# Polysketch attention and a rational feed-forward layer on one core: other product counts per unit, bfloat16 ones, and a new order from step 178 on

## The chip, the cores and the metric

The kernel runs on one core of one Trainium2 chip. A core has a matrix engine (TensorE; PE in the profile, with PEld for its weight loads), a vector engine (VectorE, DVE), a scalar engine (ScalarE, ACT), GpSimd (POOL) and SyncE (SP), and 16 DMA engines. The engines run side by side, each takes its own instructions strictly in order, and they wait for each other through semaphores. The metric is the device time of one execution, in microseconds (us); lower is better. Before the change it is 257.98 us, the median of 3 runs (257.85 to 258.45).

## The reference

Two layers. The first is linear attention with product features, for 4 batches, 4 heads, 1088 positions and head size 32:

```python
def phi(x):
    a = einsum('rd,bhsd->bhsr', S1, x)      # r = 8
    b = einsum('rd,bhsd->bhsr', S2, x)
    return einsum('bhsi,bhsj->bhsij', a, b).reshape(*x.shape[:-1], 64)
q_p, k_p = phi(q), phi(k)
kv, z = einsum('bhsf,bhsd->bhfd', k_p, v), sum(k_p, axis=2)
x = einsum('bhsf,bhfd->bhsd', q_p, kv) / (einsum('bhsf,bhf->bhs', q_p, z)[..., None] + 1e-06)
```

Its result is laid out as 4352 tokens of 128 numbers and goes through a feed-forward layer with 2048 hidden numbers per token and a rational activation:

```python
h = x @ w_in
P = a[0] + a[1] * h + a[2] * h**2 + a[3] * h**3
Q = 1.0 + abs(b[0]) * abs(h) + abs(b[1]) * h**2
out = (P / (Q + 1e-06)) @ w_out
```

## The kernel before

**Units.** The feed-forward layer is cut into 21 units (`UNITS`): a stretch of 256 or 512 tokens and some of the 16 blocks of 128 hidden numbers. Units 3 to 17 have 4096 numbers on each of 128 partitions, the others 1024 or 2048. The steps of unit i are named in a long string, `ORDER`, as a letter, the unit's number and a part:

- H: TensorE computes a 1024-wide part of h in PSUM, in fp32 (`hidden`, L511; a wide unit has four parts; the buffer `h_ps` exists twice). E copies it to SBUF as bfloat16 `hh` (`evac`, L517, on ScalarE).
- U, W, Y: u = |h| by masking the sign bit (L524), w = ab1·u + ab0 (L538), w = w·u (L553), on VectorE; then L and X on ScalarE give r = exp(-ln(w + 1 + 1e-6)), which is 1/Q (L575, L579).
- P, V, S, G on VectorE: g = a3·h + a2 (L558; on ScalarE at L561 where the step ends in `.a`), g = g·h (L571), s = h·r (L583), g = g·s (L587).
- Or, Os, Og: TensorE multiplies r, s and g with `w_out` scaled by a0, by a1 and unscaled, and adds all of it up in one PSUM tile for the token stretch (`gather`, L616). Each is one "product term", 32 matmuls of 128x128 in a wide unit.

**Three variants.** In a unit of the list `TWO` the step A adds a1 to g, so that the term with s falls away and two terms are left. The addition is a DMA that accumulates: GpSimd issues two transfers that add `ones`, a DRAM tile filled with a1, to g (`plus`, L567). In a unit of the list `FOUR` there is no P, V or G; B and C compute h²·r and h³·r (L592, L599), and four terms are summed with `w_out` scaled by a0 to a3 (w6 and w7 make two of those tables). In a unit of `SQ` (and `ABS`, the same units) ScalarE computes w = ab1·h² (D, `square`, L543, two halves) and u = ab0·|h| (L530), and the step M adds u to w by two accumulating DMAs (`join`, L549); W on VectorE and Y are absent, and so is U.

**Attention.** Steps K (keys of a batch) and Q (a stretch of queries) build the features and the result. On TensorE their steps s, sk and p write only 64 of the 128 output partitions with each matmul; they are called half-width here, and all other steps of TensorE full-width. The steps c, k, pl, kk are small copies from PSUM that run on ScalarE (`.a`) or VectorE (`.d`), f, r and x run on VectorE, b is a transpose on TensorE; dw and dr send sketches through DRAM on SP's queue.

**Order.** `ORDER` is written out by hand or by a program ahead of time and is issued step by step, under manual scheduling; so the order of the instructions on each engine, and that of SP's and GpSimd's DMAs, is the order of this string. ST copies a finished PSUM tile to SBUF (`turn_out`), OUT stores it from SP's queue (L653; the last one L645). AB prepares |b| and its root, AW writes `ones`, w0 to w5 scale and cast `w_out` in halves, Z are idle matmuls.

Of the kernel before, what the change touches and what calls it, by code (L numbers as in the profile page):

```python
# [22 lines left out]
TWO = (6, 7, 8, 10, 12, 14, 15)  # L23
SQ = (5, 9, 13)
ABS = (5, 9, 13)
FOUR = (11, 13, 16, 17)
# [3 lines left out]
WIDE = {'U': 4096, 'W': 4096, 'Y': 4096, 'V': 4096, 'S': 4096, 'G': 4096, 'L': 4096}  # L30
# [38 lines left out]
C13.0 U15.0 P15.1.d W15.0 V15.0 Y15.0 H16.0 Or13.0 H16.1 E16.0 A14.0 E16.1 X14.0 Q3.2.b H16.2 H16.3 Os13.0
Q3.2.kk.d E16.2 E16.3 L15.0 OUT10 A15.0 S14.0 U16.0.d W16.0.d G14.0 Y16.0 Or14.0 H17.0 H17.1 E17.0 E17.1 X15.0  # L70
On13.0 H17.2 H17.3 Om13.0 Og14.0 S15.0 E17.2 E17.3 U17.0.d G15.0 W17.0.d Y17.0 L16.0 H18.0 ST14.a H18.1 Or15.0
X16.0 E18.0 E18.1 L17.0 OUT14 OUT12 S16.0 X17.0 U18.0.d B16.0 W18.0.d C16.0 Y18.0 Og15.0 H19.0 Or16.0 Os16.0
Om16.0 On16.0 E19.0 L18.0 ST16.a U19.0.a X18.0 W19.0.a S17.0 B17.0 P18.0.d H20.0 C17.0 Y19.0 P19.0.a E20.0 L19.0
Or17.0 Om17.0 Os17.0 On17.0 OUT16 X19.0 ST17.a V18.0 P20.0.a U20.0.d V19.0 W20.0.d S18.0 Y20.0 S19.0 G18.0 V20.0
L20.0 Z4 Or18.0 OUT17 X20.0 Or19.0 Os18.0 Os19.0 Og18.0 Or20.0 S20.0 Os20.0 G19.0 Og19.0 G20.0 Og20.0 ST20 OUT20
# [4 lines left out]
def kernel(  # L80
# [164 lines left out]
    root1 = consts.tile([128, 1], FP, name="root1")  # L245
# [3 lines left out]
    a1, a2, a3 = a_sb[:, 1:2], a_sb[:, 2:3], a_sb[:, 3:4]  # L249
# [240 lines left out]
    def span(i, stage, k):  # L490
        w = END if i == NU - 1 and stage in "LXSG" else WIDE.get(stage, 2048)
        return k * w, min((k + 1) * w, width(i))
# [22 lines left out]
    def evac(i, part):  # L515
        c, ce = part * HW, min((part + 1) * HW, width(i))
        nc.scalar.copy(out=at(i, "hh", c, ce), in_=live[i]["h", part][:, :ce - c])  # L517
# [9 lines left out]
    def d_w(i, k, eng="d"):  # L527
        c = span(i, "W", k)
        if i in ABS:
            nc.scalar.activation(out=at(i, "u", *c), in_=at(i, "hh", *c), func=ACT.Abs, scale=ab0)  # L530
# [7 lines left out]
        nc.vector.tensor_scalar(out=at(i, "w", *c), in0=at(i, "u", *c), scalar1=ab1, scalar2=ab0,  # L538
                                op0=AX.mult, op1=AX.add)

    def square(i, k):
        c = span(i, "D", k)
        nc.scalar.activation(out=at(i, "w", *c), in_=at(i, "hh", *c), func=ACT.Square, scale=root1)  # L543
# [127 lines left out]
    def w_part(x, eng):  # L671
        if x >= 6:
            t = feature_tile(x - 6)[:, 0:4].rearrange("p t h i j -> p (t h i j)").bitcast(BF)
            t = w_sb[x - 3] = t.rearrange("p (f d) -> p f d", f=nf)
            if eng == "d":
                nc.vector.tensor_scalar(out=t, in0=w_sb[2], scalar1=a_sb[:, x - 4:x - 3], scalar2=None, op0=AX.mult)
            else:
                nc.scalar.activation(out=t, in_=w_sb[2], func=ACT.Copy, scale=a_sb[:, x - 4:x - 3])
# [7 lines left out]
        if y == 2:  # L686
            copy(eng, o, t)
        elif eng == "d":
            nc.vector.tensor_scalar(out=o, in0=t, scalar1=a_sb[:, y:y + 1], scalar2=None, op0=AX.mult)
        else:  # L690
            nc.scalar.activation(out=o, in_=t, func=ACT.Copy, scale=a_sb[:, y:y + 1])

    def written(_):
        nc.sync.dma_start(out=ones.rearrange("p (a c) -> p a c", c=128),
                          in_=a1_sb[:, None, :].broadcast_to([128, 16, 128]))

    def absolute(_):
        if TWO:
            nc.gpsimd.tensor_copy(out=a1_sb, in_=a1.broadcast_to([128, 128]))
        nc.scalar.activation(out=b_abs, in_=b_sb, func=ACT.Abs)  # L700
        if SQ:
            nc.scalar.activation(out=root1, in_=ab1, func=ACT.Ln, bias=tiny)
            nc.scalar.activation(out=root1, in_=root1, func=ACT.Exp, scale=0.5)
# [6 lines left out]
              "On": lambda i, k: gather(i, 4, k), "B": d_h2, "C": d_h3, "ST": turn_out, "OUT": store, "F": fetch, "I": early, "w": w_part, "Z": turn, "AB": absolute, "AW": written, "SS": sketch_weights}  # L710
# [44 lines left out]
```

## Time and profile before

| what | value |
|---|---|
| time, median of 3 runs | 257.98 us |
| span of the profiled execution, first to last instruction | 255.8 us |
| the profiled execution's own time | not on the page; the runs' median lies 2.2 us above the span |
| busy PE / DVE / ACT / POOL | 249.8 / 243.3 / 232.2 / 22.5 us |
| granted TensorE clock | 1.000 |
| product terms on PE (L616), share of the chain | 33.8% |
| hidden parts on PE (L511), share of the chain | 47.3% |
| accumulating transfers: `ones` into g | 14 of 512 KB, median 9.7 us from issue to landing |
| accumulating transfers: u into w | 6 of 512 KB, median 6.9 us |

The chain is the sequence of work that ended last, followed back from the last instruction; its share by line says how much of the span each line holds. Busy times of different engines overlap. A group's mean duration is the time from an instruction's start to its end; the next one on the same engine can start a little before that end. Half of PE's first 15 us are idle matmuls and short attention steps, and the last 4 us are the output's copy and store.

### The profile page before, as it was taken

How to read it: one execution, taken by the hardware profiler on the slowest of the kernel's cores; microseconds unless marked ns; L12 is line 12 of the kernel's file. 1: busy time of each engine (PE TensorE's matmuls, PEld its weight loads, DVE VectorE, ACT ScalarE, POOL GpSimd, SP SyncE). 2: the span in 40 equal slices, each digit the busy share in tenths (PEclk: the TensorE clock that was granted, in tenths of full speed). 3: DMA queues.
4: the chain of work that ended last, by engine and by line, in shares of the span. 5: the costliest groups of instructions: out<-in, count | busy, mean ns of one | idle time of the engine just before them, and what ended most of it. 6: DMA issues, size and time to landing. Idle time of an engine off the chain costs nothing.

```text
span 255.8 us, 6273 instructions
## 1 busy us (share of the span) xinstructions
PE 249.8 (98%) x2699; PEld 178.0 (70%) x2702; DVE 243.3 (95%) x242; ACT 232.2 (91%) x176; POOL 22.5 (9%) x46
## 2 busy tenths in 40 slices
PE   8999999999999999999999999999999999999993
PEld 3677746646866575666756656689566599999982
DVE  3699999999999999999999999999999999999992
ACT  2179989999999999999999999999899899999980
POOL 4000000000300040202200100220002020000000
PEclk9999999999999999999999999999999999999999
DMA  6999375649884669395995695399008575120100
GB/s 189 278 324 259 108 219 158 149 86 292 192 193 133 196 135 124 74 112 85 152 140 146 140 117 97 35 143 190 6 0 93 75 86 81 31 54 3 44 23 21
DMA packets 22618, 31.85 MB, mean 125 GB/s; under 512 B 2880, under 2 KB 15808, under 8 KB 22592
## 3 DMA queue, kind: packets, MB, share of 16 engines
q0 software_dynamic: 2880, 10.49, 30.1%
q1 hardware_dynamic: 19424, 20.90, 29.5%
q8 instruction: 21, 0.34, 0.5%
q10 hardware_dynamic: 288, 0.08, 0.1%
q14 instruction: 5, 0.04, 0.0%
HBM read 31.39 MB, written 4.26 MB: 139 GB/s over the span
## 4 chain that ended last, share of the span: by engine, by line
PE 96%; ACT 1%; DVE 0%; issue 0%; DVEq 0%
PE h_ps L511 47%; PE out_ps L616 34%; PE att_ps L426 3%; PE out_ps L197 3%; PE att_ps L330 2%; PE att_ps L454 2%; PE att_ps L299 1%; PE att_ps L366 1%; PE h_ps L376 1%; PE h_ps L299 1%; ACT hh L517 0%; ACT ln L575 0%; ACT w_out L265 0%; PE att_ps L197 0%; PE att_ps L322 0%
## 5 line engine op out<-in xcount | busy, mean ns | idle before, releaser
L511 PE MATMUL h_ps<-xT,w_in_sb 128*128 128x512 f32 (+1 forms) x320 | 126.2, 537 | 0.0
L511 PEld LDWEIGHTS h_ps<-xT,w_in_sb 128*128 128x128 f32 x320 | 57.5, 190 | 41.7 <-issue 36.6
L517 ACT CAST hh<-h_ps 128x1024 bf16<-128x1024 f32 x68 | 69.3, 1045 | 3.7 <-PE h_ps L511 2.2
L575 ACT ACTIVATE ln<-w 128x4096 f32<-128x4096 bf16 (+2 forms) x21 | 63.1, 3006 | 0.2 <-DVE w L553 0.2
L579 ACT ACTIVATE r<-ln 128x4096 bf16<-128x4096 f32 (+2 forms) x21 | 63.0, 2999 | 0.1
L583 DVE TENSOR_TENSOR s<-hh,r 128x4096 bf16<-128x4096 bf16 (+2 forms) x21 | 39.5, 1883 | 0.3 <-ACT r L579 0.2
L616 PEld LDWEIGHTS <-r 128*128 128x128 bf16 x544 | 31.7, 98 | 6.0 <-issue 5.1
L616 PEld LDWEIGHTS <-g 128*128 128x128 bf16 x544 | 31.4, 98 | 5.8 <-issue 5.1
L616 PE MATMUL out_ps<-w_out,r 128*128 128x128 bf16 x544 | 33.7, 219 | 0.0
L553 DVE TENSOR_TENSOR w<-w,u 128x4096 bf16<-128x4096 bf16 (+2 forms) x18 | 32.5, 1806 | 0.1
L571 DVE TENSOR_TENSOR g<-g,hh 128x4096 bf16<-128x4096 bf16 (+2 forms) x17 | 30.3, 1783 | 0.0
L587 DVE TENSOR_TENSOR g<-g,s 128x4096 bf16<-128x4096 bf16 (+2 forms) x17 | 30.2, 1781 | 0.0
L616 PEld LDWEIGHTS <-s 128*128 128x128 bf16 x448 | 25.9, 98 | 3.6 <-issue 3.4
L616 PE MATMUL out_ps<-w_out,g 128*128 128x128 bf16 x416 | 26.0, 219 | 0.0
L567 POOL DMA_DIRECT2D g<-ones x14 | 13.8, 1157 | 103.7 <-PE out_ps L616 39.1
L616 PE MATMUL out_ps<-w_out,s 128*128 128x128 bf16 x320 | 19.8, 219 | 0.0
L538 DVE TENSOR_SCALAR w<-u,b_abs 128x4096 bf16<-128x4096 bf16 (+2 forms) x17 | 19.3, 1136 | 0.0
L558 DVE TENSOR_SCALAR g<-hh,a_sb 128x2048 bf16<-128x2048 bf16 (+1 forms) x24 | 19.0, 793 | 0.0
L524 DVE TENSOR_SCALAR u<-hh 128x4096 uint16<-128x4096 uint16 (+2 forms) x17 | 17.3, 1015 | 0.1
L543 ACT ACTIVATE w<-hh,root 128x2048 bf16<-128x2048 bf16 x6 | 12.2, 2031 | 0.0
L549 POOL DMA_DIRECT2D w<-u x6 | 5.4, 1058 | 74.4 <-ACT u L530 74.4
L530 ACT ACTIVATE u<-hh,b_abs 128x4096 bf16<-128x4096 bf16 x3 | 11.1, 3713 | 0.0
(81 smaller groups left out, 207.1 us busy)
## 6 DMA issues: line engine op xcount, KB each, us to landing
g<-ones POOLq DMA_DIRECT2D x14, 512.0 KB, 9.7
w<-u POOLq DMA_DIRECT2D x6, 512.0 KB, 6.9
a_all<-sk_d SPq DMA_DIRECT2D x6, 352.0 KB
b_all<-sk_d SPq DMA_DIRECT2D x12, 176.0 KB
v_sb<-in_v_dram SPq DMA_DIRECT2D x12, 144.0 KB
k_sb<-in_k_dram SPq DMA_DIRECT2D x3, 544.0 KB
q_sb<-in_q_dram SPq DMA_DIRECT2D x3, 544.0 KB
out_dram<-out_sb SPq DMA_DIRECT2D x19, 64.0 KB
```

The lines of the kernel that those rows point to most:

```text
L511: nc.tensor.matmul(t[:, (x - part * m) * tl:(x - part * m + 1) * tl], lhsT=w_in_sb[:, (f0 + x) * 128:(f0 + x + 1) * 128], rhs=xT[:, p:p + ...
L517: nc.scalar.copy(out=at(i, "hh", c, ce), in_=live[i]["h", part][:, :ce - c])
L524: nc.vector.tensor_scalar(out=at(i, "u", *c).bitcast(U16), in0=at(i, "hh", *c).bitcast(U16), scalar1=0x7FFF, scalar2=None, op0=AX.bitwise_and)
L538: nc.vector.tensor_scalar(out=at(i, "w", *c), in0=at(i, "u", *c), scalar1=ab1, scalar2=ab0, op0=AX.mult, op1=AX.add)
L553: nc.vector.tensor_mul(out=at(i, "w", *c), in0=at(i, "w", *c), in1=at(i, "u", *c))
L558: nc.vector.tensor_scalar(out=at(i, "g", *c), in0=at(i, "hh", *c), scalar1=a3, scalar2=a2, op0=AX.mult, op1=AX.add)
L571: nc.vector.tensor_mul(out=at(i, "g", *c), in0=at(i, "g", *c), in1=at(i, "hh", *c))
L575: nc.scalar.activation(out=ln_sb[:, :ce - c], in_=at(i, "w", c, ce), func=ACT.Ln, bias=1.0 + 1e-6)
L579: nc.scalar.activation(out=at(i, "r", c, ce), in_=ln_sb[:, :ce - c], func=ACT.Exp, scale=-1.0)
L583: nc.vector.tensor_mul(out=at(i, "s", *c), in0=at(i, "hh", *c), in1=at(i, "r", *c))
L587: nc.vector.tensor_mul(out=at(i, "g", *c), in0=at(i, "g", *c), in1=at(i, "s", *c))
L616: nc.tensor.matmul(outs[t0][:, m * 128:(m + 1) * 128], lhsT=z[:, m * 128:(m + 1) * 128], rhs=w, start=first and j == 0 and m == 0, stop=le ...
```

## The change

- **Lists.** `TWO` goes from units 6, 7, 8, 10, 12, 14, 15 to 7 and 9 to 15; `SQ` from 5, 9, 13 to 6, 8, 10, 12, 14; `FOUR` from 11, 13, 16, 17 to 16, 17. `ABS` goes. So there are 8 x 2 + 5 x 2 = 26 accumulating transfers instead of 7 x 2 + 3 x 2 = 20.
- **Squared units.** u is now |h| from VectorE's U, unscaled, ScalarE computes only the square (one 4096-wide instruction, scaled so that w is ab1/ab0·h²), M adds them, and the factor ab0 moves into the scale operand of Ln. `RT` computes the new root, with a guard for ab0 near zero (`scale0`, on GpSimd).
- **`ones` in bfloat16.** It holds a1 rounded to bfloat16. So that the sum is still right, a2 and a3 are multiplied by rounded a1 over a1, and the unscaled table of `w_out` by the inverse (`KA0` to `KA2`: small operations on GpSimd, with one reciprocal on VectorE between them). w4 and w5 become scaled casts.
- **P** is one 4096-wide instruction instead of two halves (but for unit 3).
- **Moves.** E14.1 and E14.2 run on VectorE; some output copies, w7 and small copies change between VectorE and ScalarE.
- **Order.** The first 178 steps are the old ones with RT and KA put in behind AB; everything behind them is in another order, with parts of H in other sequences within a unit (for example H5.3, H5.2, H5.0, H5.1).

The core of the diff:

```diff
-TWO = (6, 7, 8, 10, 12, 14, 15)
-SQ = (5, 9, 13)
-ABS = (5, 9, 13)
-FOUR = (11, 13, 16, 17)
+TWO = (7, 9, 10, 11, 12, 13, 14, 15)
+SQ = (6, 8, 10, 12, 14)
+FOUR = (16, 17)
+HALF = (3,)
...
-WIDE = {'U': 4096, 'W': 4096, 'Y': 4096, 'V': 4096, 'S': 4096, 'G': 4096, 'L': 4096}
+WIDE = {'U': 4096, 'W': 4096, 'Y': 4096, 'V': 4096, 'S': 4096, 'G': 4096, 'L': 4096, 'P': 4096, 'D': 4096}
...
-K1.f0 AB0 w0.a w4.a K1.c1.d F1.q K1.f1 E0.0 U0.0 H1.0 Q0.3.sk E1.0 F1.v Q0.2.dr Q0.1.p H2.0 P0.0.d Q0.3.c.d W0.0
+Q0.0.r Q0.0.x K1.T2 Q0.2.c.a Z2 Q0.0.b K1.s1 I6 I10 Q0.2.dw Q0.1.f K1.c0.a Q0.3.T Q0.0.kk.a H0.0 w2.d K1.f0 AB0 RT0
+w0.a KA0 KA1 KA2 w4.a K1.c1.d F1.q K1.f1 E0.0.a U0.0.d H1.0 Q0.3.sk E1.0.a F1.v Q0.2.dr Q0.1.p H2.0 P0.0.d Q0.3.c.d
...
-L20.0 Z4 Or18.0 OUT17 X20.0 Or19.0 Os18.0 Os19.0 Og18.0 Or20.0 S20.0 Os20.0 G19.0 Og19.0 G20.0 Og20.0 ST20 OUT20
+V18.0 Or17.0 ST17.a U20.0.d V19.0 W20.0.d Y20.0 S18.0 Or18.0 X19.0 Or19.0 S19.0 G19.0 G18.0 OUT17 Os18.0 Og19.0
+P20.0.a V20.0 Os19.0 Og18.0 L20.0 X20.0 Or20.0 S20.0 G20.0 OUT14 Os20.0 Og20.0 ST20 OUT20
...
-        a1_sb = consts.tile([128, 128], FP, name="a1_sb")
-        ones = dram.tile([128, 2048], FP, name="ones", bufs=1)
+        a1_sb = consts.tile([128, 256], BF, name="a1_sb")
+        ones = dram.tile([128, 2048], BF, name="ones", bufs=1)
...
-        if i in ABS:
-            nc.scalar.activation(out=at(i, "u", *c), in_=at(i, "hh", *c), func=ACT.Abs, scale=ab0)
-            return
...
-        nc.scalar.activation(out=at(i, "w", *c), in_=at(i, "hh", *c), func=ACT.Square, scale=root1)
+        nc.scalar.activation(out=at(i, "w", *c), in_=at(i, "hh", *c), func=ACT.Square, scale=root)
...
-        nc.scalar.activation(out=ln_sb[:, :ce - c], in_=at(i, "w", c, ce), func=ACT.Ln, bias=1.0 + 1e-6)
+        nc.scalar.activation(out=ln_sb[:, :ce - c], in_=at(i, "w", c, ce), func=ACT.Ln, bias=1.0 + 1e-6,
+                             scale=scale0 if i in SQ else 1.0)
...
+        by = k_inv if y == 2 else a_sb[:, y:y + 1]
...
     def absolute(_):
-        if TWO:
-            nc.gpsimd.tensor_copy(out=a1_sb, in_=a1.broadcast_to([128, 128]))
         nc.scalar.activation(out=b_abs, in_=b_sb, func=ACT.Abs)
-        if SQ:
-            nc.scalar.activation(out=root1, in_=ab1, func=ACT.Ln, bias=tiny)
-            nc.scalar.activation(out=root1, in_=root1, func=ACT.Exp, scale=0.5)
+        nc.gpsimd.tensor_scalar(out=scale0, in0=ab0, scalar1=1e-12, scalar2=None, op0=AX.max)
+
+    def nearest(n):
+        if n == 0:
+            nc.gpsimd.tensor_copy(out=a1_sb, in_=a1.broadcast_to([128, 256]))
+            nc.gpsimd.tensor_scalar(out=zero, in0=a1_sb[:, 0:1], scalar1=0.0, scalar2=None, op0=AX.is_equal)
+            nc.gpsimd.tensor_add(out=near[:, 0:1], in0=a1, in1=zero)
+            nc.gpsimd.tensor_add(out=near[:, 1:2], in0=a1_sb[:, 0:1], in1=zero)
+        elif n == 1:
+            nc.vector.reciprocal(out=near_inv, in_=near)
+        else:
+            nc.gpsimd.tensor_mul(out=a_k[:, 0:1], in0=near[:, 1:2], in1=near_inv[:, 0:1])
+            nc.gpsimd.tensor_mul(out=a_k[:, 1:2], in0=near[:, 0:1], in1=near_inv[:, 1:2])
+            nc.gpsimd.tensor_mul(out=a_k[:, 2:4], in0=a_sb[:, 2:4], in1=a_k[:, 0:1].broadcast_to([128, 2]))
+
+    def square_root(_):
+        nc.scalar.activation(out=ln_b[:, 0:1], in_=scale0, func=ACT.Ln)
+        nc.scalar.activation(out=ln_b[:, 1:2], in_=ab1, func=ACT.Ln, bias=tiny)
+        nc.scalar.mul(ln_b[:, 0:1], ln_b[:, 0:1], -0.5)
+        nc.scalar.activation(out=root, in_=ln_b[:, 1:2], func=ACT.Exp, scale=0.5, bias=ln_b[:, 0:1])
```

More of the change, by code (lines that the diff above doesn't have):

```diff
@@ L69 @@
[L69 to L73, printed above, removed]
@@ L490, in span @@
     def span(i, stage, k):
[L491 removed]
+        w = END if i == NU - 1 and stage in "LXSG" else 2048 if stage == "P" and i in HALF else WIDE[stage]
         return k * w, min((k + 1) * w, width(i))
@@ L675, in w_part @@
             if eng == "d":
-                nc.vector.tensor_scalar(out=t, in0=w_sb[2], scalar1=a_sb[:, x - 4:x - 3], scalar2=None, op0=AX.mult)
+                nc.vector.tensor_scalar(out=t, in0=w_sb[2], scalar1=a_k[:, x - 4:x - 3], scalar2=None, op0=AX.mult)
             else:
-                nc.scalar.activation(out=t, in_=w_sb[2], func=ACT.Copy, scale=a_sb[:, x - 4:x - 3])
+                nc.scalar.activation(out=t, in_=w_sb[2], func=ACT.Copy, scale=a_k[:, x - 4:x - 3])
             return
@@ L685, in w_part @@
             return
[L686 to L689, printed above, removed]
+        by = k_inv if y == 2 else a_sb[:, y:y + 1]
+        if eng == "d":
+            nc.vector.tensor_scalar(out=o, in0=t, scalar1=by, scalar2=None, op0=AX.mult)
         else:
-            nc.scalar.activation(out=o, in_=t, func=ACT.Copy, scale=a_sb[:, y:y + 1])
+            nc.scalar.activation(out=o, in_=t, func=ACT.Copy, scale=by)
```

85 lines of the change are left out of this document (46 added, 39 removed).

## The prediction

> **What bounds the kernel now.** I read the page's totals first, then the table of busy time per stretch, then the chain that ended last, then single instructions around the two places that the change touches outside the main run (its head and its tail).
>
> ```profile
> span 255.8 us, 6273 instructions
> ...
> PE 249.8 (98%) x2699; PEld 178.0 (70%) x2702; DVE 243.3 (95%) x242; ACT 232.2 (91%) x176; POOL 22.5 (9%) x46
> ```
>
> Three engines are over 90% busy, so the totals do not say which one sets the end. The stretches do (window: length, then PE, PEld, DVE, ACT, POOL busy):
>
> ```profile
> 12.79:25.60 12.81, 12.65 (x127) 9.85 (x128) 12.48 (x27) 10.50 (x17) 0.00 (x0) 1.00 0.96 291
> ...
> 115.11:127.90 12.79, 12.79 (x178) 9.00 (x177) 12.79 (x12) 12.79 (x8) 3.50 (x4) 1.00 0.76 119
> ...
> 179.06:191.80 12.74, 12.74 (x99) 7.77 (x98) 12.47 (x11) 11.68 (x8) 0.07 (x1) 1.00 0.02 3
> 191.85:204.60 12.75, 12.75 (x88) 7.48 (x86) 12.72 (x9) 11.52 (x8) 1.64 (x2) 1.00 0.68 84
> ...
> 243.01:255.80 12.79, 8.50 (x135) 7.55 (x133) 8.20 (x13) 5.93 (x8) 0.00 (x0) 1.00 0.08 22
> ```
>
> From 38 to 243 us PE has no hole, DVE is idle for about 1.1 us in all, ACT for about 3.1 us, most of it in the two stretches at 179 to 205. So PE sets the end, DVE is right behind it and ACT a little further: whatever is taken from one engine is worth only what the other two can follow. The chain agrees; it is PE work laid end to end:
>
> ```profile
> 99.84 1.79 PE out_ps L616 x32
> ...
> 103.28 3.63 PE h_ps L511 x8
> 106.92 1.79 PE out_ps L616 x32
> 108.70 3.49 PE h_ps L511 x8
> ```
>
> One product term of a 4096-wide unit (32 matmuls at L616) is 1.79 us. Two hidden-layer parts (8 instructions) take 3.49 us behind a full-width step and 3.63 us behind a half-width one.
>
> The head, where the change adds instructions, and two DVE rows for the spacing:
>
> ```profile
> 16.87 1.13 ACT L691 ACTIVATE w_out<-ln,a_sb 128x1024 bf16<-128x1024 f32 x1
> 17.91 1.03 ACT L265 CAST w_out<-ln 128x1024 bf16<-128x1024 f32 x1
> 18.85 1.00 ACT L517 CAST hh<-h_ps 128x1024 bf16<-128x1024 f32 x1
> ...
> 19.99 0.42 DVE L524 TENSOR_SCALAR u<-hh 128x1024 uint16<-128x1024 uint16 x1
> ```
>
> ACT runs w0, w4 and E0.0 in a row, and DVE's U0.0 starts 0.14 us after E0.0 has ended: it waits for it. Costs of the operations (mean ns last before the idle column):
>
> ```profile
> L558 DVE TENSOR_SCALAR g<-hh,a_sb 128x2048 bf16<-128x2048 bf16 x23 | 18.5, 804 | 0.0
> L538 DVE TENSOR_SCALAR w<-u,b_abs 128x4096 bf16<-128x4096 bf16 x12 | 16.1, 1341 | 0.0
> L524 DVE TENSOR_SCALAR u<-hh 128x4096 uint16<-128x4096 uint16 x12 | 14.7, 1221 | 0.1
> L543 ACT ACTIVATE w<-hh,root 128x2048 bf16<-128x2048 bf16 x6 | 12.2, 2031 | 0.0
> L530 ACT ACTIVATE u<-hh,b_abs 128x4096 bf16<-128x4096 bf16 x3 | 11.1, 3713 | 0.0
> L592 DVE TENSOR_TENSOR g<-s,hh 128x4096 bf16<-128x4096 bf16 x4 | 9.2, 2289 | 0.0
> ```
>
> Neighbours overlap by 0.09 us on DVE (a product that starts at 204.18 is followed at 206.38, 2.20 us later, though it lasts 2.29) and by 0.10 on ACT, so I count a product as 2.20, U as 1.14, W as 1.25, half a P as 0.72, an evacuation as 0.95, Abs as 3.6, half a square as 1.93.
>
> **The change, engine by engine.** PE: units with two products go from seven to eight (7, 9 to 15), with four from four to two (16, 17). Among the 15 wide units that was 7x2 + 4x4 + 4x3 = 42 terms and becomes 8x2 + 2x4 + 5x3 = 39: three terms fewer, 3 x 1.79 = -5.4 us. Grouping: I counted the unbroken runs of half-width steps in both orders: 19 before, 18 after. A run costs about 0.15 us on the way in (Q.p for three tiles 0.85 us instead of 0.70 in the chain) and 0.14 on the way out, so -0.3 us. Hidden parts, attention steps and idle matmuls (Z) are the same in number.
>
> DVE, in us: U in three more units (the squared units now take it) +3.4; W in two fewer -2.5; Y in two fewer -4.4; V and G in two more (units 11, 13) +8.8; B and C in two fewer -8.8; P from 10 units at 2 x 0.72 to 12 at one 4096-wide instruction, priced as W's 1.25 (same operation and shape), +0.6; two evacuations of unit 14 moved here +2.4 (by the PSUM copies, 0.385 us for 256 and 0.690 for 512, some 1.2 for 1024); the smaller moves (three output copies, w7 and P18 to ACT, three key copies, P19 and Q3.0.kk back, three xT copies away, den steps, one reciprocal) -2.7. Sum -3.2.
>
> ACT: three Abs away -10.8; squares from 6 x 1.93 to five 4096-wide at 3.64 (the 4096-wide Abs) +6.6; two evacuations away -1.9; output copies +1.3; w7 +1.85 (as a 2048-wide row); P18 and P19 +0.9; xT copies +0.75; small copies -0.4; a per-partition scale on five Ln and on w4, w5 +0.6 (the scaled w0 took 1.13 us where plain w4 took 1.03); two more root steps +0.4. Sum -0.7. ACT is hardly relieved.
>
> POOL and the queues: 26 accumulating transfers instead of 20, each two issues of about 1 us on an engine that is 9% busy; the extra 6 cost POOL time that nobody waits for. `ones` becomes bfloat16, so an A transfer reads half as much and should land like an M (median 6.9 us, not 9.7). SP: OUT14, with 6 stores, is now behind OUT17. Stores issue 0.43 us apart, OUT17's began at 245.5, so 10 of them end near 249.8 before any shift, ahead of the last store's 251.95: no cost; without that 2 us of cover it would delay the end by up to 2.6.
>
> **The head.** RT0 puts two more tiny ACT steps and a POOL round trip (scale0) ahead of w0.a; dependent tiny ACT steps are 0.32 us apart (16.44, 16.76), so w0 starts near 17.4 instead of 16.87. w4.a now waits for KA2: POOL's chain of small operations (0.1 to 0.3 us each by its rows), then a reciprocal on DVE that queues behind K1.f0 until 18.3, then three POOL multiplies, so about 18.95 instead of 17.91. Queued behind w4 are E0.0 (end 20.95 instead of 19.85) and E1.0, which today waits 0.40 us for PE and swallows that much. ACT, packed from 21 us on, runs +0.65; U0.0 waits, DVE +0.9; PE takes the +0.65 over near 28 us, where it already waits for ACT's kvz copy. Bounds: 0 (added steps give nothing back) and +1.1, with every POOL step at the 0.29 of its 128-wide copy. I take 0.65, since the short rows are the nearer ones.
>
> **The tail.** After the last X, DVE still has two G; now S20 and one G, -0.6 us for DVE and ACT's end. PE needs no credit.
>
> **Sum.** PE -5.4 - 0.3 + 0.65 = -5.0. DVE -3.2 + 0.9 - 0.6 = -2.9, or -4.0 if its 1.1 us of idle closes. ACT -0.7 + 0.65 - 0.6 = -0.65, or -3.75 if all 3.1 us of its idle closes. So ACT decides. Its idle at 179 to 205 (1.06 + 1.23 us) lay where PE worked off the four-product units 11 and 13 and kept it waiting for h_ps. Those are gone: for a pair of units 10 to 15 (one squared, one not) PE now needs 2 x (6.97 + 3.58) = 21.1 us and ACT 25.4, so ACT is not starved there; I close these 2.3 us and leave the other 0.8. Then -0.65 - 2.3 = -2.95 on the span of 255.8, that is 252.85. The page gives no time for the profiled execution but its span; the median of 257.98 lies 2.2 us above it, which the change doesn't touch: 257.98 - 2.95 = 255.0 us. Bounds of the sum: with the head at 0 and all ACT idle closed -4.4, with the head at 1.1 and none closed -0.2.
>
> **A rule against it.** POOL's issue rows while DVE was full:
>
> ```profile
> L549 POOL DMA_DIRECT2D w<-u x6: 857/1100/1220, 66.8 to 171.2; - x6
> ...
> DMA to landing us min/median/max: 4.6/6.9/9.1
> ```
>
> The two issues of one A ran from 145.85 to 147.61 across a DVE product that began at 146.51 and lasted 2.29, and neither was late. The Trainium skill (SBUF — State Buffer, "Who interferes with whom") states that a DVE operation in a two-port mode and a GpSimd operation lock each other out for a whole instruction, descriptor writing included. By that rule the held POOL of rival 3 would be the normal case, and the time 262.2 instead of 255.0; the trace does not agree in this place, and the landings above were taken beside a full DVE, so the sum goes by the rows.
>
> **Rivals.** (1) PE alone decides: ACT finds work all the time, the head hides. -3.75 to -5.0, so 254.2 to 253.0. For it: in the new order PE's work summed up to each step (rows times counts) stays ahead of DVE's by 2 to 8 us and of ACT's by 2 to 12. Against it: ACT would have to run without a hole from 21 us to the end. (2) ACT's holes only move (fewer hidden parts ready, a wait for DVE's Y instead): -0.65 to 0, so 257.3 to 258. Against: 25.4 against 21.1. (3) Slower: the joins land late. Five Ln now wait for an M on the fullest engine. Between the end of D and its Ln the order has 11.5 (unit 6), 11.4, 11.4, 10.1 (unit 12) and 11.4 us of ACT work. M needs one issue plus a landing: 1.1 + 6.9 at the median, 10.2 at the slowest M, but 13.5 at the slowest A row (12.4). At that row units 12 and one other stall 3.4 + 2.1 = 5.5 us, so 255.0 + 5.5 = 260.5; it decides from some 3 us of such stalls on. Against: 6.9 leaves 2 us spare. The same would come about if POOL were held for a whole product at each issue: 1.1 + 6.9 + 2 x 2.29 = 12.6 us, 7.2 us of stalls over the five, 262.2; the issues from 145.85 speak against it, and it has 0.02 of this rival's chance. (4) The grouping does nothing: 0.3 us, inside all the others.
>
> **How the numbers follow.** Forecast 0.50, with its own range 254.2 to 256.4; rival 1 0.20; rival 2 (up to 258.3) 0.16; rival 3 0.14. A measurement here tells about 0.2%, 0.5 us, from no change. Faster by more (under 257.5): 0.50 + 0.20 + 0.07 of rival 2 = 0.77; the same 0.09; slower 0.14. Range: 253.0, rival 1's end, to 258.2, rival 2's.
>
> **What would show it.** PE's L616 rows 96 matmuls fewer and PE's holes some 2 us in all after 38; ACT's busy time about 231.5 and no hole over 0.5 us between 150 and 215; P at 4096 in one row near 1.34; the Ln of units 6, 8, 10, 12, 14 with no DMA ahead of it; E0.0 starting near 20.0. Wrong if a wait for w (a join) or for g (ones) shows ahead of Ln or G, if ACT waits for h_ps as long as before, or if the head costs over 1.1.

## The result and the profile after

| | changed kernel | the same again | kernel before beside them |
|---|---|---|---|
| median time | 255.99 us (5 runs, 255.07 to 256.81) | 255.30 us (6 runs, 254.87 to 255.59) | 258.02 and 257.67 us |
| ratio to before, 95% interval | 0.9918 [0.9890, 0.9946] | 0.9898 [0.9876, 0.9920] | 1 |
| span of the profiled execution | 253.3 us (its time 255.07) | 253.1 us (its time 254.87) | 255.8 us |

The change makes the kernel faster by 0.8 to 1.0%, that is by 2.0 to 2.4 us on the medians. The forecast was 255.0 us with an own range of 254.2 to 256.4: both medians lie in it, 0.3 and 1.0 us above the forecast.

The changed kernel's page, its span, its busy time per engine and its chain by engine:

```profile
span 253.3 us, 6086 instructions
...
PE 244.4 (96%) x2603; PEld 172.1 (68%) x2606; DVE 240.1 (95%) x229; ACT 231.9 (92%) x179; POOL 32.9 (13%) x59
...
PE 38%; ACT 21%; DVE 19%; issue 13%; DMA 6%; SPq 1%; ACTq 0%; DVEq 0%
```

PE has lost 5.4 us of work, DVE 3.2, ACT 0.3, and the span only 2.5. The chain was PE to 96% before. Now it is PE from some 30 to 113 us (ahead of that it runs over loads and attention steps) and then changes hands, as its pieces in order of time (start, length, what) show:

```profile
109.42 1.79 PE out_ps L618 x32
111.21 1.79 PE h_ps L518 x4
113.05 0.59 DVE s L585
...
118.87 2.10 DVE g L572
120.97 2.30 DVE w L554
...
130.77 3.52 ACT ln L576
...
135.07 3.63 ACT r L581
```

The table by stretch for the changed kernel (window: length, then PE, PEld, DVE, ACT, POOL busy). The first two rows cut the main run in two, the others are the places where ACT was starved before and where it is now:

```profile
38.40:115.00 76.60, 76.60 (x767) 49.66 (x766) 76.02 (x71) 74.61 (x58) 6.33 (x6) 1.00 0.59 148
115.00:205.00 90.00, 88.98 (x866) 58.92 (x866) 89.06 (x67) 89.76 (x56) 21.57 (x20) 1.00 0.71 138
...
179.06:191.80 12.74, 12.69 (x115) 8.44 (x115) 12.74 (x9) 12.74 (x7) 4.51 (x4) 1.00 0.45 86
191.85:204.60 12.75, 12.54 (x116) 8.37 (x114) 12.56 (x8) 12.75 (x10) 3.59 (x5) 1.00 1.04 197
51.16:63.90 12.74, 12.74 (x98) 7.14 (x96) 12.74 (x14) 11.59 (x11) 0.00 (x0) 1.00 0.42 130
63.95:76.70 12.75, 12.75 (x161) 8.43 (x159) 12.75 (x12) 12.09 (x11) 0.00 (x0) 1.00 0.52 130
```

At 179 to 205 ACT now runs without a hole, where it was idle for 2.3 us before. But at 51 to 77 it is idle for 1.15 + 0.66 = 1.8 us, where before it was idle for 0.03. PE is still full there, and ACT waits for its hidden parts; ACT's instructions in that place (start, length, what, idle time before):

```profile
52.10 3.62 ACT L581 ACTIVATE r<-ln 128x4096 bf16<-128x4096 f32 x1 [0.26 <-PE out_ps L618]
...
58.90 1.01 ACT L272 CAST hh<-h_ps 128x1024 bf16<-128x1024 f32 x1 [0.69 <-PE h_ps L518]
...
66.45 1.01 ACT L272 CAST hh<-h_ps 128x1024 bf16<-128x1024 f32 x1 [0.49 <-PE h_ps L518]
```

**A ledger on ACT.** The two profiles can be cut at three ACT instructions: the |b| step, the first copy of a hidden part (E0.0) and the end of the last exponential. The forecast's terms fall into the same pieces (the 2.95 of the sum, with E0.0 1.1 later as it worked out, leave 3.45 for the long piece).

| piece | before | after | measured | forecast |
|---|---|---|---|---|
| start to the \|b\| step | 16.14 | 15.37 | -0.77 | 0 |
| \|b\| to E0.0 | 2.71 | 3.77 | +1.06 | +1.1 |
| E0.0 to the end of the last exponential | 230.14 | 228.13 | -2.01 | -3.45 |
| from there to the end | 6.81 | 6.03 | -0.78 | -0.6 |
| span | 255.80 | 253.30 | -2.50 | -2.95 |

The first piece holds the same steps in both kernels. In 14 profiles of kernels of this family the |b| step starts anywhere between 14.75 and 16.73 us; the ten idle matmuls at the start alone take 3.62 to 4.45 us. I put nothing of it down to the change, and why it varies stays open. That is a choice: the two profiles of the old kernel and its variant have the step at 16.14 and 15.88, later than eleven of the twelve of the changed kernel and its variants (14.75 to 15.66; in the twelfth, 16.73, PE waits 1.08 us for VectorE behind a late load), so a part of the 0.77 may be the change's. Below I use, beside the medians, the time from the |b| step to the end: 239.7 us before, 237.9 after (237.7 in the second set). Counted so, the change gives 1.8 to 2.0 us. This time comes from one execution of each kernel (two of the changed one, 0.2 apart), so a few tenths of a us in it show nothing either.

The long piece misses 1.4 us. ACT's busy time in it fell by 0.81 (225.35 to 224.54), and its idle time by 1.20 instead of the 2.75 that I had taken for it (2.3 at 179 to 205 and 0.45 at E1.0).

### The profile page after: what moved, and what is told of

Its sections match the earlier page's. It is cut to its first block, busy times and chain, and to the rows that moved or that the text cites. A ratio compares the mean times of both kernels' runs of the same rounds, so it can differ in the third digit from the quotient of the medians.

```text
span 253.3 us, 6086 instructions
## 1 busy us (share of the span) xinstructions
PE 244.4 (96%) x2603; PEld 172.1 (68%) x2606; DVE 240.1 (95%) x229; ACT 231.9 (92%) x179; POOL 32.9 (13%) x59
## 3 DMA queue, kind: packets, MB, share of 16 engines
q0 software_dynamic: 3744, 13.63, 29.2%
## 4 chain that ended last, share of the span: by engine, by line
PE 38%; ACT 21%; DVE 19%; issue 13%; DMA 6%; SPq 1%; ACTq 0%; DVEq 0%
PE h_ps L518 20%; PE out_ps L618 10%; ACT r L581 6%; ACT ln L576 6%; ACT hh L272 5%; DVE g L589 3%; DVE w L554 3%; DMA v_sb<-in_v_dram 3%; DVE s L585 3%; PE att_ps L337 3%; PE att_ps L433 2%; DVE g L594 2%; DVE g L572 2%; DMA k_sb<-in_k_dram 2%; DVE w L539 2%
## 5 line engine op out<-in xcount | busy, mean ns | idle before, releaser
L576 ACT ACTIVATE ln<-w 128x4096 f32<-128x4096 bf16 (+2 forms) x16 | 44.9, 2803 | 0.0
L589 DVE TENSOR_TENSOR g<-g,s 128x4096 bf16<-128x4096 bf16 (+2 forms) x19 | 34.7, 1837 | 0.1
L572 DVE TENSOR_TENSOR g<-g,hh 128x4096 bf16<-128x4096 bf16 (+2 forms) x19 | 34.7, 1834 | 0.0
L618 PE MATMUL out_ps<-w_out,g 128*128 128x128 bf16 x480 | 29.8, 219 | 0.1
L550 POOL DMA_DIRECT2D w<-u x10 | 12.3, 1359 | 133.3 <-ACT w L544 74.2
L554 DVE TENSOR_TENSOR w<-w,u 128x4096 bf16<-128x4096 bf16 (+2 forms) x16 | 28.0, 1750 | 0.1
L618 PEld LDWEIGHTS <-s 128*128 128x128 bf16 x352 | 20.6, 98 | 5.3 <-issue 4.0
L576 ACT ACTIVATE ln<-w,scale 128x4096 f32<-128x4096 bf16 x5 | 18.8, 3759 | 0.0
L544 ACT ACTIVATE w<-hh,root 128x4096 bf16<-128x4096 bf16 x5 | 18.6, 3726 | 0.1
L559 DVE TENSOR_SCALAR g<-hh,a_k 128x4096 bf16<-128x4096 bf16 (+2 forms) x16 | 18.5, 1168 | 0.0
```

Of the source, the lines that this page charges most:

```text
L554: nc.vector.tensor_mul(out=at(i, "w", *c), in0=at(i, "w", *c), in1=at(i, "u", *c))
L572: nc.vector.tensor_mul(out=at(i, "g", *c), in0=at(i, "g", *c), in1=at(i, "hh", *c))
L589: nc.vector.tensor_mul(out=at(i, "g", *c), in0=at(i, "g", *c), in1=at(i, "s", *c))
L618: nc.tensor.matmul(outs[t0][:, m * 128:(m + 1) * 128], lhsT=z[:, m * 128:(m + 1) * 128], rhs=w, start=first and j == 0 and m == 0, stop=le ...
```

## Experiments

Two theories stood at the start. Mine: the three engines now bind together, each for some stretch, so that relief of one of them is soon stopped by the next. The rival: one engine (PE, or ACT by the forecast) decides, and its relief alone shows in the time. The next four kernels relieve one engine each, then all three. They leave out a part of the computation and serve only to weigh an engine. The reliefs lie in different units, so each speaks for the places where it lies and not for the whole run. The changed kernel stands at 255.99 and 255.30 us, and at 237.9 and 237.7 from |b| on.

### PE alone

The terms with s of units 4, 6 and 8 are left out: 96 matmuls, 5.4 us of PE.

```diff
-K3.T2 K3.T1 Os4.0 H7.2 Q2.1.dr
+K3.T2 K3.T1 H7.2 Q2.1.dr
...
-H9.2 G5.0 Os6.0 S7.0
+H9.2 G5.0 S7.0
...
-H12.2 Os8.0 H12.3
+H12.2 H12.3
```

> The changed kernel with the s terms of units 4, 6 and 8 left out on TensorE (96 matmuls at the gather line, 3 x 1.79 = 5.4 us of PE work; the output lacks them). My theory: after the change PE no longer sets the end; from about 113 us on the chain runs over ACT and DVE, so the span falls by 0 to 1.2 us only (time 254.8 to 256.0). Rival, PE still sets the end as its 96% busy share suggests: the span falls by 4 to 5.4 us (250.6 to 252.0).

Measured: 255.17 us, 0.9893 [0.9862, 0.9923]; from |b| on 237.7. Taking 5.4 us from the engine with the most work gains 0.0 to 0.2 us from |b| on and 0.1 to 0.8 by the medians, as my theory had it. PE's idle time between 38 and 243 us grows from 1.8 to 5.8 us, most of it spent waiting for ACT (who waits, for whom: us, times, longest; from 38 to 243 us):

```profile
PEld h_ps L518 <- ACT hh L272: 5.1, 8, 1.3
...
PE h_ps L518 <- ACT hh L272: 2.4, 4, 0.7
PE out_ps L618 <- ACT out_sb L272: 2.2, 2, 1.9
```

The three terms stand at 75, 109 and 149 us in the changed kernel, where ACT has next to no idle time. At 51 to 67 us, where ACT does stand idle behind a full PE, PE was not relieved.

### ACT alone

The logarithm of units 5, 9 and 13 covers half of each unit: 5.1 us of ACT.

```diff
+        if i in (5, 9, 13):
+            ce = c + 2048
```

> The changed kernel with Ln of units 5, 9 and 13 done on the first half of their columns only (3 x 1.7 = 5.1 us of ACT work left out, the other half of r is wrong). My theory, ACT decides with DVE close behind: the span falls by 1.5 to 3.5 us (252.5 to 254.5). Rival, PE decides: 0 to 0.5 us. Rival, DVE alone decides: 0 to 0.5 us here, and a fall in the run that relieves DVE.

Measured: 254.66 us, 0.9873 [0.9838, 0.9907]; from |b| on 236.9. That is 0.8 to 1.0 us from |b| on, less than expected, but the most of the three. The chain is PE and DVE again, and ACT waits for both products of PE:

```profile
PE 54%; DVE 26%; issue 10%; ACT 8%; POOL 0%; DVEq 0%; ACTq 0%
```

```profile
ACT hh L272 <- PE h_ps L518: 3.3, 4, 1.6
ACT r L583 <- PE out_ps L620: 1.9, 4, 0.8
```

### DVE alone

V covers half of units 5, 7, 9, 11 and 13: 5.3 us of DVE.

```diff
+        if i in (5, 7, 9, 11, 13):
+            c = (c[0], c[0] + 2048)
```

> The changed kernel with the product V of units 5, 7, 9, 11 and 13 done on half the columns (5 x 1.07 = 5.3 us of DVE work left out, their g is wrong there). My theory, ACT decides and DVE is close behind: the span falls by 0.3 to 1.5 us (254.5 to 255.7). Rival, DVE decides: 2.5 to 5 us (251 to 253.5). Rival, PE decides: 0 to 0.3.

Measured: 255.29 us, 0.9901 [0.9864, 0.9938]; from |b| on 238.0: nothing. Of the 5.3 us, 4.7 are now waits for ACT's r:

```profile
DVE s L587 <- ACT r L583: 4.7, 6, 1.1
```

### All three

The three edits together.

> The changed kernel with all three reliefs at once: the s terms of units 4, 6, 8 left out on TensorE (5.4 us), Ln of units 5, 9, 13 and V of units 5, 7, 9, 11, 13 on half their columns (5.1 us of ACT, 5.3 us of DVE). Theory, after the single reliefs gave 0.7 to 1.3 us each: the three engines bind together, each taking over where another is relieved; then the time falls by 3.5 to 5 us (251.0 to 252.5). Rival, something that belongs to none of the three (transfers landing late, buffers) holds the end: 1 to 2 us (254 to 255).

Measured: 252.84 us, 0.9804 [0.9782, 0.9825]; from |b| on 235.0. That is 2.5 to 3.2 us by the medians (2.7 to 3.4 by the medians of the spans) and 2.7 to 2.9 from |b| on, where the three singles add up to 0.8 to 1.2. That is less than I had expected (251.0 to 252.5), and more than the rival's 1 to 2 us. So no one engine decides at the places of these reliefs, and relief is worth something where it falls on all three. It is still far from 5.1; I put the rest down to the order, which sets who waits for whom, but no run shows that apart.

### PE alone in the kernel before

The same 96 matmuls are taken from the old kernel (the terms with s of units 4, 5 and 9).

```diff
-E8.0 Os4.0 Og4.0
+E8.0 Og4.0
...
-D9.0 Os5.0 H9.2
+D9.0 H9.2
...
-H13.2 Os9.0 E13.1
+H13.2 E13.1
```

> The kernel before with the s terms of units 4, 5 and 9 left out on TensorE: the change's saving of 96 matmuls (5.4 us of PE) alone. Theory of the prediction, PE set the end but DVE was 1.1 us and ACT 3.1 us of idle time behind it: the time falls by 1.0 to 2.0 us (256.0 to 257.0) and DVE and ACT wait less. Rival, PE alone set the end: 4 to 5.4 us (252.6 to 254). Rival, PE's full row was a matter of waiting in the pipeline: 0 to 0.5 us.

Measured: 257.18 us, 0.9978 [0.9962, 0.9994], so 0.6 us (0.2 to 1.0) faster than before, some 0.2 of it outside the span (see "The time outside the span" below); from |b| on it is 240.2 against 239.7, which shows no gain at all. I had expected 1.0 to 2.0 us; the last rival's 0 to 0.5 is the nearest. In this kernel, too, PE then waits for ACT:

```profile
PEld h_ps L511 <- ACT hh L517: 8.1, 7, 2.5
PE h_ps L511 <- ACT hh L517: 4.5, 3, 1.6
```

Before the change PE had no hole between 38 and 243 us and made up 96% of the chain, and yet these 5.4 us of its work were worth next to nothing alone. The three terms stood at 91, 107 and 160 us, and from 64 to 165 us ACT was idle for 0.01 us in all: as full as PE. So "PE sets the end" in the prediction's first part was a wrong reading of these views, for this part of the run at least; "ACT decides" in its sum was the better one. At 179 to 205 us, where ACT stood idle beside a full PE, PE alone was not relieved.

### The head

KA0 goes behind I8, KA1 and KA2 behind K1.T1, RT0 between H3.1 and E3.1, all to places where their engines have room.

```diff
-K0.p0 I8 F1.k
+K0.p0 I8 KA0 F1.k
...
-K1.s0 K1.T1 Q0.1.c.a
+K1.s0 K1.T1 KA1 KA2 Q0.1.c.a
...
-AB0 RT0
-w0.a KA0 KA1 KA2 w4.a
+AB0
+w0.a w4.a
...
-H3.1 E3.1.a
+H3.1 RT0 E3.1.a
```

> The changed kernel with the head's new steps moved off the path: KA0 right behind the loads (I8), KA1 and KA2 behind K1.T1, RT0 between H3.1 and E3.1 where ACT waits 0.70 us for PE anyway; nothing left out. My theory, the head costs what the trace shows (E0.0 starts 3.77 us behind the start of |b| instead of 2.71): E0.0 comes 1.0 us earlier against |b|, DVE's wait of 0.78 us ahead of U0.0 goes, and the time falls by 0.6 to 1.1 us (254.9 to 255.4). Rival, the delay is swallowed by ACT's idle at 51 to 77 us: the time falls by 0 to 0.2 us and the waits there grow.

Measured: 254.64 us, 0.9872 [0.9840, 0.9905]; from |b| on 237.2, 0.5 to 0.7 less than the changed kernel. The head of the changed kernel on ACT:

```profile
15.37 0.21 ACT L699 ACTIVATE b_abs<-b_sb 128x2 f32<-128x2 f32 x1
15.92 0.20 ACT L716 ACTIVATE ln_b<-scale 128x1 f32<-128x1 f32 x1 [0.35 <-POOL scale L700]
...
16.64 1.13 ACT L692 ACTIVATE w_out<-ln,a_sb 128x1024 bf16<-128x1024 f32 x1
18.09 1.15 ACT L692 ACTIVATE w_out<-ln,a_k 128x1024 bf16<-128x1024 f32 x1 [0.32 <-POOL a_k L712]
19.14 1.91 ACT L272 CAST hh<-h_ps 128x1024 bf16<-128x1024 f32 x2
```

and with the steps moved:

```profile
15.66 0.21 ACT L699 ACTIVATE b_abs<-b_sb 128x2 f32<-128x2 f32 x1
15.77 1.14 ACT L692 ACTIVATE w_out<-ln,a_sb 128x1024 bf16<-128x1024 f32 x1
16.81 1.14 ACT L692 ACTIVATE w_out<-ln,a_k 128x1024 bf16<-128x1024 f32 x1
18.05 1.01 ACT L272 CAST hh<-h_ps 128x1024 bf16<-128x1024 f32 x1
```

From |b| to E0.0 it is 3.77 us in the first and 2.39 in the second: 1.38 us earlier, of which 0.71 is lost again at E1.0, which waits for PE. What is left, some 0.67, is what the time from |b| on shows. By the medians it is 0.7 to 1.35 us, so the small steps that now run ahead of |b|, where the time from |b| on does not see them, cost nothing that shows.

### The changed kernel a second time

The kernel as it is, with no edit: how far do two sets of runs differ?

> The changed kernel once more, unchanged, beside the two below, since its five runs lay 1.7 us apart (255.07 to 256.81) and the single reliefs of 0.7 to 1.3 us are read against them. If its median is that of the kernel: 255.5 to 256.5. If those five were on the slow side: 255.0 to 255.5, and the gains of a_head and of the single reliefs shrink by as much.

Measured: 255.30 us, 0.9898 [0.9876, 0.9920]. It is 0.7 us below the first set, and both intervals overlap: the first set lay high, which is the second of the two cases that I had set out. So differences of 0.7 us between single sets mean little here, and where the text rests on less it uses the time from |b| on or an instruction that has moved.

### w7 on DVE

The kernel of "The head", with the scaling of a table (w7) on DVE, as it was before the change.

```diff
-Og7.0 w7.a U12.0.d
+Og7.0 w7.d U12.0.d
```

> The changed kernel with the head's steps moved as in a_head, and w7 on DVE again (0.72 us there instead of 2.06 us on ACT) so that the output copy of unit 8, which waits behind it and for which PE waits 1.04 us at 160.7, comes 2 us earlier. Theory, ACT and DVE bind together around 150 to 205 us: 0.2 to 0.9 us faster than a_head (253.7 to 254.4). Rival, the relief of ACT is eaten by DVE's 0.65 us: no difference to a_head (254.5 to 254.8), PE's wait goes all the same.

Measured: 253.82 us, 0.9848 [0.9825, 0.9871]; from |b| on 236.4. In the changed kernel w7 takes 2.06 us on ACT ahead of an output copy (ST8), and PE stands for it:

```profile
161.16 1.95 PE L618 MATMUL out_ps<-w_out,r 128*128 128x128 bf16 x32 [0.76 <-ACT out_sb L272]
```

That wait is gone. In its place ACT waits 0.78 for PE at 161.22 and PE's weights wait 1.21 for DVE at 173; what is left is 0.8 us from |b| on. This is the fastest kernel of the study with the whole computation, 1.5% under before: its interval lies below both of the changed kernel's.

### E14 on ACT

As "w7 on DVE", and the copies of two hidden parts of unit 14, which the change had moved to DVE, go back to ACT.

```diff
-H14.1 E14.1.d Q3.2.p
+H14.1 E14.1.a Q3.2.p
...
-Q3.2.r E14.2.d Q3.2.x
+Q3.2.r E14.2.a Q3.2.x
```

> a_w7 (head's steps moved, w7 on DVE) with the evacuations E14.1 and E14.2 on ACT again: ACT +1.9 us, DVE -2.5 us. In a_w7 TensorE waits 0.38 us, and its weight loads 1.67 us, for these two on DVE at 171 to 174 us. Theory, ACT and DVE bind equally there: those waits go and the time stays within 0.6 us of a_w7 (253.2 to 254.4). Rival, ACT is the tighter one: 0.6 to 1.9 us slower (254.4 to 255.7). Rival, DVE is the tighter one: 0.6 to 1.5 us faster (252.3 to 253.2).

Measured: 255.55 us, 0.9916 [0.9893, 0.9939]; from |b| on 238.4. My expectation was wrong, the rival's right: 1.9 us more on ACT (two copies at 0.95) make the kernel 1.7 us slower by the medians and 2.0 from |b| on, though DVE has 2.4 us less to do (two copies of 1.2). DVE waits for ACT:

```profile
DVE s L585 <- ACT r L581: 2.3, 3, 1.3
```

So around unit 14 (170 to 200 us) ACT is the tightest engine of the three: work moved from it to DVE pays nearly in full there.

### ones in fp32

The changed kernel with `ones` in fp32 again (its values are still a1 rounded to bfloat16; the lines that fill it are left out here).

```diff
-        ones = dram.tile([128, 2048], BF, name="ones", bufs=1)
+        ones = dram.tile([128, 2048], FP, name="ones", bufs=1)
```

> The changed kernel with the ones tile in fp32 again (the rounded a1, so that the sums are the same; nothing left out). Theory from the trace after: bfloat16 ones did not bring the landing down (9.6 us against 9.7 before), because a landing here is mostly waiting on the 16 DMA engines and not reading; so the median landing stays within 9.0 to 11.5 us, the queue's share of the engines rises by a few per cent, and the time moves by less than 0.4 us. Rival, as the prediction had it, the read halves the transfer: landing 12 us or more, and G waits for it, 0.5 to 3 us slower.

Measured: 256.26 us, 0.9943 [0.9924, 0.9963]; from |b| on 239.1, 1.2 to 1.4 more than with bfloat16. Landing (KB each, median us from issue to landing), first in this kernel, then in the changed one:

```profile
g<-ones POOLq DMA_DIRECT2D x16, 512.0 KB, 13.4
w<-u POOLq DMA_DIRECT2D x10, 512.0 KB, 6.5
```

```profile
g<-ones POOLq DMA_DIRECT2D x16, 512.0 KB, 9.6
w<-u POOLq DMA_DIRECT2D x10, 512.0 KB, 6.0
```

I had expected 9.0 to 11.5 for fp32 and less than 0.4 us of time; the rival was right: the median is 13.4, and G waits for it:

```profile
DVE g L590 <- DMA g<-ones: 2.6, 3, 1.5
```

With 14 such transfers before, fp32 landed at 9.7. So with 26 accumulating transfers the smaller type is needed to stand still, and it is worth 0.3 to 1.0 us by the medians.

### The tail

As "w7 on DVE", with PE's term Or17 ahead of On17, where ACT's r has long been there.

```diff
-Om17.0 C17.0 P18.0.a
+Om17.0 Or17.0 C17.0 P18.0.a
...
-V18.0 Or17.0 ST17.a
+V18.0 ST17.a
```

> a_w7 with Or17 ahead of On17 on TensorE, so that the PSUM tile of unit 17 is full one term earlier and Or17 fills the 0.43 us in which TensorE waits for C17. In a_w7 TensorE waits 0.43 us (for C17) and 0.56 us (for the output copy of unit 17) at 237 to 242. Theory, the end is held by ACT's and DVE's last steps: both waits go and the time changes by less than 0.3 us. Rival, TensorE holds the end there: 0.5 to 1.0 us faster (252.8 to 253.3).

Measured: 253.94 us, 0.9853 [0.9825, 0.9882]; from |b| on 236.4, the same. PE's wait of 0.43 us for s is gone, and its wait for the output copy grew from 0.6 to 1.2: a wait that only moved.

### Unit 8 with two terms

As "w7 on DVE", with unit 8 in `TWO` as well: one more pair of transfers, one term (1.79 us of PE) fewer.

```diff
-TWO = (7, 9, 10, 11, 12, 13, 14, 15)
+TWO = (7, 8, 9, 10, 11, 12, 13, 14, 15)
...
-W9.0.d V8.0 Og6.0
+W9.0.d V8.0 A8.0 Og6.0
...
-H12.2 Os8.0 H12.3
+H12.2 H12.3
```

> a_w7 with unit 8 in TWO as well: A8 (two more accumulating transfers) behind V8, Os8 gone, so 32 matmuls (1.79 us of TensorE) fewer around 157 us, nothing left out of the result. TensorE, DVE and ACT are each busy for 88.6 to 89.7 of the 90 us from 115 to 205 in a_w7, and ACT waits 0.78 us for TensorE's products at 161. Theory, the three bind together and a relief of one is worth a sixth of itself or so, as with the 5.4 us of a_pe3: 0 to 0.5 us faster than a_w7 (253.3 to 253.9). Rival, TensorE is the tightest there now: 1.0 to 1.8 us faster (252.0 to 252.8). Rival, the two more transfers land late or hold up another: slower by 0.5 us or more (254.3 and up).

Measured: 254.73 us, 0.9863 [0.9828, 0.9899]; from |b| on 236.7 against 236.4. No gain: by the medians it is 0.9 us slower, as the rival with late transfers had it, but the intervals of the two overlap. A join now lands late:

```profile
ACT ln L576 <- DMA w<-u: 0.8, 1, 0.8
```

This is the prediction's third rival in small, with one more pair in the queue. Since the late join came together with the relief, this run does not say what 1.79 us of PE alone are worth here.

## Why the prediction was right, and where it was not

**What bounds the kernel.** Wrong in its words, harmless in its sum. "PE sets the end" fell, for 64 to 165 us, with the kernel before without 96 matmuls (0.6 us for 5.4). "Whatever is taken from one engine is worth only what the other two can follow" was right, and the three single reliefs and the joint one show it.

**The sum by engine.** PE's busy time fell by 5.4 and DVE's by 3.2, both as summed. ACT's fell by 0.3 instead of 0.7, a sum of many small moves. It had a double count, too: the two root steps (0.4) stood in it and in the head. The rows agree with their prices: P in one piece 1.335 us (priced as 1.341), the copy on DVE 1.225 (1.2), the square 3.73, the scaled logarithm 3.76 against 3.68, w7 2.06.

```profile
L559 DVE TENSOR_SCALAR g<-hh,a_k 128x4096 bf16<-128x4096 bf16 x12 | 15.8, 1335 | 0.0
```

**"ACT decides."** Right for a part of the run: two copies moved back to ACT cost 1.7 us, and ACT is the one engine whose relief alone shows. But 5.1 us of ACT gained 0.8 to 1.0 only, so it is not all of it.

**"I close these 2.3 us and leave the other 0.8."** This is the step that failed. The 2.3 us at 179 to 205 closed in full, but ACT got 1.8 us of new idle time at 51 to 77, where PE is still full, so its idle time between 38 and 243 went from 3.2 (read as 3.1) to 2.3 instead of 0.8. That the forecast was met all the same is in part luck: the long piece missed 1.4 us, and the first piece, which it held to be the same, gave 0.8 back.

The reason given for the 2.3 us was right only for one half, too. The kernel before's waits of ACT's copies (us, times, longest):

```profile
ACT hh L517 <- PE h_ps L511: 2.2, 4, 0.7
...
ACT hh L517 <- DVE s L599: 1.2, 1, 1.2
```

The hole at 180 to 182 us, 1.06 us in two pieces, is a wait for `h_ps`, as said. The one at 198 to 199, 1.23 us, is put down to VectorE: the step C of unit 13, which reads `hh`, ends at 198.95, and the copy starts at 199.32. Both belong to the four-product units, so both went with them; that it was the lists and not the new order that closed them was not tried apart.

The new holes are the second rival's mechanism (the holes move), at a place where I had not looked: the pairs of units that I reckoned PE's and ACT's need for were units 10 to 15 only. The lists hold a hint that I passed over: units 6 and 8 get a term more (two to three), units 9, 11 and 13 lose 1, 2 and 2, so the relief of PE lies late. Whether this makes the early holes was not tried: the terms that were left out for PE lie behind them, and the holes stood there unchanged (0.69 and 0.49).

**The head.** Right. E0.0 came 1.06 later (1.1 by the long rows, 0.65 after E1.0's wait), and moving the steps away gave back 0.5 to 0.7 from |b| on. E1.0 swallowed the 0.40 as said; but the exponential X0.0 still came 1.06 later (0.83 in the second profile, where PE has no wait of 0.32 us for a load at 25.7), so the 0.40 was not kept all the way.

**The tail.** Right: -0.78 after the last exponential for -0.6. OUT14 behind OUT17 shows no cost.

**`ones` "should land like an M".** Wrong: 9.6 us median, as before, not 6.9. It was a term without a price, and the wait that it could have caused did not come, since the order leaves room (no G waits for `ones` in the changed kernel). Without the smaller type it would have come: 2.6 us of waits.

**The third rival, late joins.** Refuted for this kernel: no Ln waits for a join, and the joins' landing of 6.0 us is shorter than before's 6.9. But POOL is held by DVE, as the last section shows, in a way that the prediction had judged too lightly.

**The time outside the span.** I took 2.2 us, the distance of the median to the profiled span, as something that the change doesn't touch. The changed kernel's profiled execution took 255.07 for a span of 253.3, so for it the time outside is 1.8, as in all its eleven runs (1.74 to 1.84). The runs of the kernel before beside the later sets have 1.87 to 2.09, on average 1.96 to 1.99. So some 0.2 of the 2.0 to 2.4 us that the medians show lies outside the span, ahead of the first instruction or behind the last. The old kernel without its 96 matmuls has 1.77 on average, too, so this 0.2 does not seem to hang on the new lists or the new order; what makes it stays open. Two sets have single executions with more ("PE alone" up to 2.3, "All three" up to 2.9). With 1.8 the forecast for the profiled execution would have been 254.65, 0.4 below what it took.

**What would show it.** PE's holes after 38 were to be some 2 us: between 115 and 243 they are 1.02 + 0.80. ACT's busy time was to be about 231.5 (231.9), without a hole over 0.5 between 150 and 215 (none), no join ahead of an Ln (none), E0.0 near 20.0 (19.14, with |b| 0.77 earlier).

## What to carry to other kernels

An engine that has no hole and makes up the whole chain need not be what binds: where three engines are over 90% busy, take a few microseconds from each alone and from all together, in every stretch that matters (here 0.0 to 0.2, 0.8 to 1.0, 0 and 2.7 to 2.9 for some 5 us each) before one of them is given a price. When a change shifts relief to a part of the run, reckon each engine's need stretch by stretch from the first unit on, also where nothing seems to change; idle time that closes in one place can open in another. And set-up steps belong where their engine has room: a dozen tiny operations ahead of the first unit cost 0.5 to 0.7 us here, and nothing that shows when moved.

## What was not expected of the hardware

**GpSimd's issues and VectorE.** The prediction held the lock of the Trainium skill (SBUF — State Buffer, "Who interferes with whom") against one place of the trace, where two issues ran beside a two-input product and were not late. That place could not test it, and "the trace does not agree" was a wrong reading. The same section of the Trainium skill says that `tensor_scalar` can enter a two-port mode and that `tensor_tensor` has none, and the product is a TENSOR_TENSOR. The first of the two issues lay mostly beside a TENSOR_SCALAR (W, 145.25 to 146.59); it ended at 146.72 after 0.87 us, which shows no hold and rules none out. The kernel before had a clearer place, behind a row that the prediction did not show (shortest, median and longest, in ns):

```profile
L567 POOL DMA_DIRECT2D g<-ones x14: 858/1059/1992, 93.2 to 205.3; - x14
```

The two issues from 93.19 on end at 94.60 and 95.90, 0.08 and 0.12 us behind a half P (until 94.52) and W (until 95.78), both TENSOR_SCALAR. In the changed kernel more such neighbours show. GpSimd's issues at 129.68 and 139.61, and VectorE beside the first:

```profile
129.68 3.13 POOL L550 DMA_DIRECT2D w<-u  x2 [19.12 <-ACT w L544]
139.61 5.01 POOL L568 DMA_DIRECT2D g<-ones  x4 [6.80 <-DVE g L572]
```

```profile
129.76 1.36 DVE L559 TENSOR_SCALAR g<-hh,a_k 128x4096 bf16<-128x4096 bf16 x1
...
131.33 1.36 DVE L559 TENSOR_SCALAR g<-hh,a_k 128x4096 bf16<-128x4096 bf16 x1
```

The two issues of the first row last 1.57 us each and end at 131.25 and 132.81, 0.13 and 0.12 us behind the ends of the two P instructions (131.12 and 132.69); beside products an issue lasts 0.86 to 0.89. Of the four in the second row, the one from 141.22 lasts 3.40 us and ends at 144.62, behind U, w6 and W in a row, whose last ends at 144.54. So the lock of the Trainium skill shows here beside 2-byte operations with one tensor input, and does not beside 2-byte products of two tensors, as its section has it. Held issues cost no time in this kernel: no Ln waits for a join and no G for `ones`. By the mechanism they would, where a join is due soon and VectorE runs U, W and P back to back; no run here shows that.

**Landing times grow with the queue.** The same 512 KB from fp32 `ones` landed in 9.7 us with 20 accumulating transfers in the kernel and in 13.4 with 26. The landing goes with what the queue's packets take of the 16 DMA engines' span: 30.1% in the kernel before (9.7 us), 29.2% in the changed one (9.6), 36.9% with fp32 (13.4). That the one makes the other is an argument from three kernels, not shown.
